# Linear attention and a bilinear FFN on one core: the order of the first units' work, and state updates moved beside the intra matmuls

## The chip, the core and the metric

The kernel runs on one core of a Trainium2 chip. The metric is device time in microseconds (us). One core has five engines that matter here: TensorE (PE in the profile; PEld are its weight loads), VectorE (DVE), ScalarE (ACT), GpSimd (POOL), and SyncE (SP), from whose queue nearly all DMAs are issued.

## The reference

The first half is decayed linear attention over 4 batches, 8 heads, 768 positions and head size 64, in blocks. The second half takes its result, as 3072 rows of 512, through a bilinear feed-forward layer (FFN).

```python
for b in range(nb):
    intra = np.einsum('bhic,bhjc->bhij', qb, kb) * Dmask[None]
    intra = np.einsum('bhij,bhjd->bhid', intra, vb)
    inter = np.einsum('bhid,bhde->bhie', qb * lam_pow[None], kv_state)
    out[:, :, sl] = intra + inter
    kb_dec = kb * rev_pow[None]
    kv_state = lam_block[None, :, None, None] * kv_state + np.einsum('bhsd,bhse->bhde', kb_dec, vb)
...
a = x @ w_a
b = x @ w_b
return (a * b @ w_out).astype(np.float32)
```

`Dmask` is lam to the power of the distance on and below the diagonal, and zero above it.

## The kernel before

**Units.** The kernel uses blocks of 128 positions, so each batch has NB = 6 blocks, and a block of one batch with all 8 heads is a unit; there are 24. q is multiplied by lam^pos and k by lam^-pos (tables lp_q and lp_k), so that the decay needs no factor in the state, which is then a plain sum of k times v over a batch's earlier units. The mask that remains is a triangle of ones (`lotri`). Heads are handled in pairs (HP = 4 pairs), 128 rows for two heads.

**The pieces of a unit.**
- `prep_k` and `prep_v` (L273, L285; P, or PK and PV, in the plan): scale q and k into `qk`, cast v into `vb`; from unit 11 on a DMA transpose on SP's queue makes `qkT`, before that `piece_T` (L289, T) does it on TensorE with a ScalarE copy. They also issue later loads (`pump`).
- `scores` (L302): k times q for each head, 16 matmuls of half the rows for two units, into two PSUM banks `kq` per unit; `masks` (L312, VectorE, L320): two multiplies by the triangle per unit, bank by bank. Both together are `piece_S` (S).
- `inter` (L330): the state `st` of the unit before times q, four matmuls; `intra` (L339): masked scores times v, eight matmuls of 64 output rows (two heads fill the two halves of the array); both add into the bank `o_ps`. `evac_o` (L349, ScalarE as a rule) copies it into `xT`, the FFN's input.
- `piece_V` (L387, V): `kv_update` (L367) adds k times v of the unit to the batch's state in the bank `kvd`, with four 128x128 matmuls (two heads by two heads), of which the two diagonal 64x64 blocks are used. `kv_copy` (L374) then copies it into `st` with a multiply by `bdiag`, which zeroes the other two blocks (VectorE, L381). The last unit of a batch has no update.
- `pieces_O` (L394; O, O2, Q in the plan): outputs of one or two units. Q also takes one or two later units `nxt`, whose scores are put between inter and intra; their masks are issued last.

**The FFN** (`ffn`, L437) works on groups of 4, 1, 2, 4, 4, 4, 4 and 1 units (GROUPS). For each of FC = 12 slices of d_ff, `a_part` (L417) makes four matmuls into a bank a_ps and a ScalarE copy, `b_part` (L423) four into b_ps and a VectorE multiply (`ab`, L425). Then each 128 rows of output take 12 matmuls (op, L434), a ScalarE copy and a store. After slice f it calls `hook(f)`; in the output part `hook(12 + 2t)` and `hook(13 + 2t)` after the first and the second half of tile t. These are the slots. What is issued in a slot stands in PLAN (L39), written out by hand: group, then (slot, piece, unit). The order within each engine is the program's order (manual scheduling), so the attention of later units is woven into the FFN of earlier ones on every engine's queue.

**Banks.** `ps_bank` (L105) hands out seven PSUM banks in rotation; FFN allocations skip the bank that the last FFN allocation took:

```python
i = bank["next"]
while i in bank["held"] or (ffn and i == bank["ffn"]):
    i = (i + 1) % 7
if ffn:
    bank["ffn"] = i
bank["next"] = (i + 1) % 7
```

A new tile in a bank waits for the readers of the tile before it. The eighth bank is that of `kvd` (and of the idle matmuls of `warm`, L192, which keep TensorE active at the start).

**The first four units** (the packed start, L487 to L582) come before any FFN. q and k of four units are loaded in a packed layout, four head pairs in two parts; `load4` (L497) scales a part on VectorE (L503), transposes it on TensorE (L508), and `unpack` (L516) copies it out on ScalarE (L517). For k the two halves of a part go into one bank, and each is unpacked by itself. `scores4` (L533) makes the scores of four units for a part (L542) and then their masks, `natural_k` (L521) transposes k back for the state updates, and `kv_mms` (L356) builds the states of units 0 to 2 in three banks at once. Then follow intra, inter and evacuations of the four units, and the FFN of group 0.

Of the kernel before, what the change touches and what calls it, by code (L numbers as in the profile page):

```python
# [17 lines left out]
BF16 = mybir.dt.bfloat16  # L18
# [4 lines left out]
def _bc(ap, dims):  # L23
# [9 lines left out]
PACK = 4  # L33
# [16 lines left out]
}  # L50
for _g, _u in ((3, 11), (4, 15), (5, 19)):
    PLAN.setdefault(_g, []).extend(
        [(1, "V", _u - 1), (1, "P", _u + 2), (3, "P", _u + 3), (4, "V", _u),
         (7, "Q", (_u, _u + 1, _u + 2, _u + 3)), (10, "V", _u + 1), (10, "P", _u + 4),
         (12, "P", _u + 5), (13, "V", _u + 2), (16, "Q", (_u + 2, _u + 3, _u + 4, _u + 5))])
PLAN[5] = [(_s, _n, (21, 22, 23) if _us == (21, 22, 23, 24) else _us)
           for _s, _n, _us in PLAN[5] if _us != 24]
PLAN[6] = [(1, "V", 22), (4, "O", 23)]


@with_exitstack
def kernel(
# [11 lines left out]
    nc = tc.nc  # L74
    B, H, S, D = q.shape
    BLK = 128
    NB = S // BLK
    HP = H // 2
# [26 lines left out]
    def ps_bank(name, shape, dt, hold=False, ffn=False):  # L105
# [6 lines that stand above are left out]
        if hold:  # L112
            bank["held"].add(i)
        return ps_pool.tile(shape, dt, name=name, tag=f"ps{i}")
# [19 lines left out]
    staged = {}  # L134
# [32 lines left out]
    n0 = GROUPS[0]  # L167
# [24 lines left out]
    def warm(n, cols=128):  # L192
        for _ in range(n):
            nc.tensor.matmul(idle_ps[:, :cols], lhsT=idle_sb[:, :128], rhs=idle_sb[:, :cols],  # L194
                             start=True, stop=True, skip_group_check=True)
# [5 lines left out]
    x4 = {}  # L201
    for w, src in (("q", q), ("k", k)):
        x4_r = src[0, :, 0:PACK * BLK, :].rearrange("h (p r) d -> p h (r d)", r=PACK)
        for i in range(2):
            t = wst_pool.tile([128, 1024], F32, name=w + "4", tag="wst")
# [42 lines left out]
    U = {}  # L248
# [81 lines left out]
    def inter(u):  # L330
        d = U[u]
        if u % NB > 0:
            first = o_bank(u)
            for hp in range(HP):
                nc.tensor.matmul(d["o"][:, hp, :], lhsT=st_bufs[(u - 1) % 4][:, hp, :, :],  # L335
                                 rhs=d["qT"][:, hp, :], start=(first and hp == 0), stop=True,
                                 skip_group_check=True)

    def intra(u):  # L339
        d = U[u]  # L340
        first = o_bank(u)
        for hp in range(HP):
            for i in range(2):
                p = slice(64 * i, 64 * i + 64)
                nc.tensor.matmul(d["o"][p, hp, :], lhsT=d["vb"][:, 2 * hp + i, :],  # L345
                                 rhs=d["m"](i, hp), start=(first and hp == 0),
                                 stop=True, skip_group_check=True)

    def evac_o(u, xT, col, eng="act"):  # L349
        o_ps = U[u].pop("o")  # L350
        if eng == "act":
            nc.scalar.copy(xT[:, :, col:col + BLK], o_ps)  # L352
        else:
            nc.vector.tensor_copy(xT[:, :, col:col + BLK], o_ps)

    def kv_mms(ps, w, hps, first):  # L356
        d = U[w]
        for hp in hps:
            nc.tensor.matmul(ps[:, hp, :, :], lhsT=d["kn"][:, 2 * hp:2 * hp + 2, :],  # L359
                             rhs=d["vb"][:, 2 * hp:2 * hp + 2, :], start=(first and hp == 0),  # L360
                             stop=True, skip_group_check=True)
# [5 lines left out]
    def kv_update(u):  # L367
        if u % NB == NB - 1:
            return
        if u % NB == 0:  # L370
            kv_bank()
        kv_mms(kv["ps"], u, range(HP), u % NB == 0)

    def kv_copy(u, ps, eng="dve"):  # L374
        st = st_bufs[u % 4]
        if eng == "act":
            for i in range(2):
                p = slice(64 * i, 64 * i + 64)
                nc.scalar.copy(st[p, :, i, :], ps[p, :, i, :])  # L379
        else:  # L380
            nc.vector.tensor_mul(st[:].rearrange("p hp i d -> p hp (i d)"),  # L381
                                 ps[:].rearrange("p hp i d -> p hp (i d)"), bdiag_bc)
# [11 lines left out]
    def pieces_O(us, nxt=()):  # L394
        kqs = [score_banks() for u in nxt]
        for u in us:
            inter(u)
        for u, kq in zip(nxt, kqs):
            scores(u, kq)
        for u in us:  # L400
            intra(u)
            xT, col = xTs[u]
            evac_o(u, xT, col)
        for u, kq in zip(nxt, kqs):
            masks(u, kq)

# [87 lines left out]
    xT4 = {"q": scr[0][:, 4:8, :], "k": scr[1][:, 4:8, :]}  # L494
    kn4 = scr[1][:, 8:12, :].rearrange("p u (h d) -> p u h d", d=D)

    def load4(w, i, parts):  # L497
        dst = xs4[w].rearrange("p r (h d) -> p r h d", d=D)
        tab = lp_q if w == "q" else lp_k
        tps = ps_bank("t" + w, [128, 2, PACK, 128], BF16)  # L500
        for j in range(2):
            hs = slice(4 * i + 2 * j, 4 * i + 2 * j + 2)
            nc.vector.tensor_mul(  # L503
                dst[:, :, hs, :].rearrange("p r h d -> p h r d"),
                x4[w, i][:, :, 2 * j:2 * j + 2].rearrange("p r h d -> p h r d"),
                tab[:, NB:, hs, :].rearrange("p r h o -> p h r o").to_broadcast([128, 2, PACK, D]))
            for r in range(PACK):
                nc.tensor.transpose(tps[:, j, r, :],  # L508
                                    xs4[w][:, r, hs.start * D:hs.stop * D], ident)
            if parts == 2:  # L510
                unpack(i, tps, slice(j, j + 1), w)
        staged.pop((w + "4", i))
        if parts == 1:
            unpack(i, tps, slice(0, 2), w)

    def unpack(i, tps, js, w):  # L516
        nc.scalar.copy(xT4[w][:, 2 * i + js.start:2 * i + js.stop, :]  # L517
                       .rearrange("c hp (p r) -> c hp p r", r=PACK),
                       tps[:, js].rearrange("c j r p -> c j p r"))

    def natural_k(us, hps):  # L521
        nu, nh = len(us), len(hps)
        tps = ps_bank("tn", [128, nu, nh, 128], BF16)
        for a, u in enumerate(us):
            for b, hp in enumerate(hps):
                nc.tensor.transpose(tps[:, a, b, :], xT4["k"][:, hp, u * BLK:(u + 1) * BLK], ident)
        nc.scalar.copy(kn4[:, us[0]:us[0] + nu, 2 * hps[0]:2 * (hps[0] + nh), :]
                       .rearrange("p u h d -> p u (h d)"),
                       tps[:].rearrange("p u j x -> p u (j x)"))

    ms4 = {}

    def scores4(i):  # L533
        kqs = []
        for up in range(PACK // 2):
            kq = score_banks()
            for uu in range(2):
                cols = slice((2 * up + uu) * BLK, (2 * up + uu + 1) * BLK)
                for j in range(2):
                    for par in range(2):  # L540
                        p = slice(64 * par, 64 * par + 64)
                        nc.tensor.matmul(kq[par][:, 2 * uu + j, :],  # L542
                                         lhsT=xT4["k"][p, 2 * i + j, cols],
                                         rhs=xT4["q"][p, 2 * i + j, cols],
                                         start=True, stop=True, skip_group_check=True)
            kqs.append(kq)
        for up, kq in enumerate(kqs):
            ms4[i, up] = mask(kq)

    for u in range(n0):  # L550
        U[u] = dict(kn=kn4[:, u], qT=xT4["q"][:, :, u * BLK:(u + 1) * BLK],
                    m=lambda i, hp, u=u: ms4[hp // 2, u // 2][i][:, 2 * (u % 2) + hp % 2, :])
    for w, parts in (("q", 1), ("k", 2)):
        for i in range(2):
            load4(w, i, parts)
            if w == "q":
                warm(4)
    for u in range(n0):
        make_vb(u, "pool")
    scores4(0)  # L560
    natural_k((0, 1, 2), (0, 1))
    natural_k((0, 1, 2), (2, 3))
    scores4(1)
    sts = [ps_bank("kv0", [128, HP, 2, D], F32), ps_bank("kv1", [128, HP, 2, D], F32), kv_bank()]
    for hh in range(2):
        for u, ps in enumerate(sts):
            for w in range(u + 1):
                kv_mms(ps, w, range(2 * hh, 2 * hh + 2), w == 0)
            if hh:
                kv_copy(u, ps, ("act", "act", "dve")[u])  # L570
    intra(0)
    evac_o(0, *xTs[0])
    intra(1)
    inter(1)
    evac_o(1, *xTs[1])
    intra(2)
# [73 lines left out]
```

## Time and profile before

| | |
|---|---|
| median of 18 runs | 238.84 us (237.87 to 242.3) |
| the profiled execution's own time | 238.44 us |
| its span, first to last instruction | 236.7 us |
| granted TensorE clock, mean | 0.989 |
| TensorE, VectorE, ScalarE busy | 228.1, 115.7, 92.7 us |
| first FFN matmul starts | 20.38 us |
| FFN matmuls a_ps, b_ps, op | 77.1, 77.2, 65.6 us |
| masks (VectorE, L320) | 48 instructions, mean 682 ns |
| state copies (VectorE, L381) | 18 instructions, mean 684 ns |

A timeline line has the start in us, the length in us, the engine, the line of the kernel, the instruction with what it writes and reads, and the number of like instructions merged into it; in brackets is idle time ahead of it and what ended it. The end of a matmul is modelled, so the start of the next one is the better measure of its cost. The chain of waits is followed back from the last instruction to whatever released each step.

### The profile page before, as it was taken

How to read it: one execution, taken by the hardware profiler on the slowest of the kernel's cores; microseconds unless marked ns; L12 is line 12 of the kernel's file. 1: busy time of each engine (PE TensorE's matmuls, PEld its weight loads, DVE VectorE, ACT ScalarE, POOL GpSimd, SP SyncE). 2: the span in 40 equal slices, each digit the busy share in tenths (PEclk: the TensorE clock that was granted, in tenths of full speed). 3: DMA queues.
4: the chain of work that ended last, by engine and by line, in shares of the span. 5: the costliest groups of instructions: out<-in, count | busy, mean ns of one | idle time of the engine just before them, and what ended most of it. 6: DMA issues, size and time to landing. Idle time of an engine off the chain costs nothing.

```text
span 236.7 us, 4519 instructions
## 1 busy us (share of the span) xinstructions
PE 228.1 (96%) x1761; PEld 126.7 (54%) x1761; DVE 115.7 (49%) x205; ACT 92.7 (39%) x174; POOL 49.2 (21%) x63
## 2 busy tenths in 40 slices
PE   7689999998999999999999999999999999999993
PEld 2375444458698754454544454544454544444493
DVE  0875656646658637675135665135564214332050
ACT  3558555046464542342143242242341233431161
POOL 6050000245346354103305403003300000000000
PEclk9979999999999999999999999999999999999998
DMA  4999999999989999996929969523120220000311
GB/s 151 302 289 348 348 367 271 295 212 288 232 193 217 204 222 228 238 175 100 226 87 216 182 78 231 139 74 80 25 47 0 89 89 4 0 0 18 118 44 48
DMA packets 94278, 38.32 MB, mean 162 GB/s; under 512 B 81200, under 2 KB 89776, under 8 KB 94256
## 3 DMA queue, kind: packets, MB, share of 16 engines
q1 hardware_dynamic: 94112, 38.02, 70.1%
q8 instruction: 14, 0.23, 0.4%
q14 instruction: 8, 0.07, 0.1%
q10 hardware_dynamic: 144, 0.00, 0.0%
HBM read 28.32 MB, written 6.29 MB: 146 GB/s over the span
## 4 chain that ended last, share of the span: by engine, by line
PE 88%; SPq 4%; ACT 2%; DMA 2%; issue 1%; DVE 1%; POOL 0%; DVEq 0%; ACTq 0%
PE a_ps L413 27%; PE b_ps L413 26%; PE op L434 26%; SPq L125 3%; PE o_ps L345 2%; DMA vf<-in_v_dram 2%; PE kq L308 2%; PE kvd L359 2%; PE o_ps L335 1%; PE tps L294 1%; ACT xT L352 1%; SPq L206 1%; ACT o_sb L429 1%; ACT st L379 1%; PE kv L359 0%
## 5 line engine op out<-in xcount | busy, mean ns | idle before, releaser
L425 DVE TENSOR_TENSOR ab<-a_sb,b_ps 128x512 bf16<-128x512 bf16 (+2 forms) x96 | 52.7, 553 | 82.5 <-PE b_ps L413 60.2
L413 PE MATMUL a_ps<-xT,wa_sb 128*128 128x512 bf16 (+2 forms) x384 | 77.1, 326 | 1.2 <-ACT xT L352 0.6
L413 PE MATMUL b_ps<-xT,wb_sb 128*128 128x512 bf16 (+2 forms) x384 | 77.2, 326 | 0.0
L420 ACT CAST a_sb<-a_ps 128x512 bf16<-128x512 f32 (+2 forms) x96 | 45.6, 481 | 66.1 <-PE a_ps L413 65.7
L434 PE MATMUL op<-wo_sb,ab 128*128 128x512 bf16 (+2 forms) x312 | 65.6, 363 | 0.0
L413 PEld LDWEIGHTS <-wb_sb 128*128 128x128 bf16 x384 | 34.5, 98 | 28.8 <-issue 0.2
L413 PEld LDWEIGHTS <-wa_sb 128*128 128x128 bf16 x384 | 33.6, 98 | 28.1 <-issue 1.4
L434 PEld LDWEIGHTS <-ab 128*128 128x128 bf16 x312 | 28.6, 98 | 30.2
L320 DVE TENSOR_TENSOR m<-kq,lotri 128x512 bf16<-128x512 f32 x48 | 29.9, 682 | 21.9 <-PE kq L308 20.4
L256 POOL TENSOR_TENSOR qk<-kf,lp_k 128x512 bf16<-128x512 f32 x17 | 17.9, 1052 | 78.1 <-issue 33.2
L429 ACT COPY o_sb<-op 128x512 f32<-128x512 f32 (+2 forms) x26 | 14.2, 554 | 37.2 <-PE op L434 37.2
L261 POOL TENSOR_TENSOR qk<-qf,lp_q 128x512 bf16<-128x512 f32 x20 | 22.9, 1144 | 24.5 <-DMA qf<-in_q_dram 24.5
L352 ACT CAST xT<-o_ps 128x512 bf16<-128x512 f32 x23 | 12.4, 590 | 16.4 <-PE o_ps L345 16.4
L381 DVE TENSOR_TENSOR st<-kvd,bdiag 128x512 bf16<-128x512 f32 x18 | 12.3, 684 | 3.8 <-PE kvd L359 3.8
L296 ACT COPY qkT<-tps 128x1024 bf16<-128x1024 bf16 x7 | 7.1, 1012 | 11.2 <-PE tps L294 11.2
L270 DVE CAST vb<-vf 128x512 bf16<-128x512 f32 x17 | 8.6, 503 | 0.0
L345 PE MATMUL o_ps<-m,vb 128*64 128x128 bf16 x192 | 7.8, 222 | 0.0
L194 PE MATMUL idle<-idle_sb 128*128 128x512 bf16 (+1 forms) x21 | 6.3, 465 | 1.3 <-DVE idle_sb L189 1.3
L270 POOL CAST vb<-vf 128x512 bf16<-128x512 f32 x7 | 4.3, 614 | 15.3 <-DMA vf<-in_v_dram 12.5
L335 PEld LDWEIGHTS <-st 128*128 128x128 bf16 x80 | 5.4, 98 | 2.8
L308 PE MATMUL kq<-qkT 64*128 64x128 bf16 x160 | 6.6, 218 | 0.0
L345 PEld LDWEIGHTS <-vb 128*64 128x64 bf16 x192 | 5.7, 109 | 1.3
(52 smaller groups left out, 86.5 us busy)
## 6 DMA issues: line engine op xcount, KB each, us to landing
vf<-in_v_dram SPq DMA_DIRECT2D x24, 256.0 KB, 5.0
out_dram<-o_sb SPq DMA_DIRECT2D x23, 256.0 KB, 2.2
qf<-in_q_dram SPq DMA_DIRECT2D x20, 256.0 KB, 4.4
kf<-in_k_dram SPq DMA_DIRECT2D x20, 256.0 KB, 4.9
wst<-in_moe_w_a_dram SPq DMA_DIRECT2D x6, 512.0 KB, 8.9
wst<-in_moe_w_b_dram SPq DMA_DIRECT2D x6, 512.0 KB, 9.0
wst<-in_moe_w_out_dram SPq DMA_DIRECT2D x6, 512.0 KB, 8.7
q<-in_q_dram SPq DMA_DIRECT2D x2, 512.0 KB, 5.6
```

The costliest lines, as they stand in the source:

```text
L256: eng_of(eng).tensor_mul(qk[:, 1], raw.pop((u, "k")), lp_k[:, u % NB].to_broadcast([128, H, D]))
L261: eng_of(eng).tensor_mul(U[u]["qk"][:, 0], raw.pop((u, "q")), lp_q[:, u % NB].to_broadcast([128, H, D]))
L270: eng_of(eng).tensor_copy(vb, vf)
L320: nc.vector.tensor_mul(m, kq[i], lotri_bc)
L345: nc.tensor.matmul(d["o"][p, hp, :], lhsT=d["vb"][:, 2 * hp + i, :], rhs=d["m"](i, hp), start=(first and hp == 0), stop=True, skip_group_c ...
L352: nc.scalar.copy(xT[:, :, col:col + BLK], o_ps)
L381: nc.vector.tensor_mul(st[:].rearrange("p hp i d -> p hp (i d)"), ps[:].rearrange("p hp i d -> p hp (i d)"), bdiag_bc)
L413: nc.tensor.matmul(ps[:, :gt], lhsT=w_sb[:, s, f * 128:(f + 1) * 128], rhs=xT[:, s, :gt], start=(s == 0), stop=(s == KS - 1))
L420: nc.scalar.copy(a_sb[:, :gt], ps[:, :gt])
L425: nc.vector.tensor_mul(ab[:, f, :gt], a_sb[:, :gt], ps[:, :gt])
L429: nc.scalar.copy(o_sb[:, lo:hi], op[:, lo:hi])
L434: nc.tensor.matmul(op[:, lo:hi], lhsT=ab[:, f, t * 128:(t + 1) * 128], rhs=wo_sb[:, f, lo:hi], start=(f == 0), stop=(f == FC - 1))
```

## The change

In the packed start, each half of a part of k gets a bank of its own and is transposed and unpacked by itself (`part_k`), with three idle matmuls of 128 columns after each of the first three halves. The first part's scores (`scores4` now takes the pairs of units to do) come ahead of the last half's transposes, and two idle matmuls after each `natural_k`. The second part's scores are issued in two steps among the state matmuls, the banks of the first two states being taken before them, and the last six state matmuls for unit 2 with its copy come after intra of unit 1.

From unit 7 on, when `pieces_O` outputs two units, the second one's state update (`kv_beside`) is issued right after their intra matmuls and ahead of the masks of `nxt`. It writes only the two diagonal blocks, with eight matmuls of 128 rows, 64 output rows and 64 columns, except for the first unit of a batch, which keeps the four full ones. The V pieces of units 8, 10, 12, 14, 16, 18, 20 and 22 leave the plan, and the S pieces of units 11 and 12 move from slot 2 to slot 3.

```diff
     2: [(0, "V", 6), (1, "T", 7), (1, "P", 8), (4, "T", 8), (5, "P", 9), (6, "S", 7),
-        (6, "S", 8), (7, "V", 7), (8, "P", 10), (9, "T", 9), (10, "V", 8), (11, "T", 10),
+        (6, "S", 8), (7, "V", 7), (8, "P", 10), (9, "T", 9), (11, "T", 10),
...
-    3: [(2, "S", 11), (2, "S", 12)],
+    3: [(3, "S", 11), (3, "S", 12)],
...
-        [(1, "V", _u - 1), (1, "P", _u + 2), (3, "P", _u + 3), (4, "V", _u),
-         (7, "Q", (_u, _u + 1, _u + 2, _u + 3)), (10, "V", _u + 1), (10, "P", _u + 4),
+        [(1, "P", _u + 2), (3, "P", _u + 3), (4, "V", _u),
+         (7, "Q", (_u, _u + 1, _u + 2, _u + 3)), (10, "P", _u + 4),
...
-PLAN[6] = [(1, "V", 22), (4, "O", 23)]
+PLAN[6] = [(4, "O", 23)]
...
+    def kv_beside(u):
+        if u % NB == 0 or u % NB == NB - 1:
+            kv_update(u)
+        for hp in range(HP if 0 < u % NB < NB - 1 else 0):
+            for i in range(2):
+                p = slice(64 * i, 64 * i + 64)
+                nc.tensor.matmul(kv["ps"][p, hp, i, :], lhsT=U[u]["kn"][:, 2 * hp + i, :],
+                                 rhs=U[u]["vb"][:, 2 * hp + i, :],
+                                 start=False, stop=True, skip_group_check=True)
+        if u % NB < NB - 1:
+            kv_copy(u, kv["ps"])
...
             evac_o(u, xT, col)
+        if len(us) == 2 and us[0] >= n0 + 3:
+            kv_beside(us[1])
         for u, kq in zip(nxt, kqs):
             masks(u, kq)
...
-    for w, parts in (("q", 1), ("k", 2)):
-        for i in range(2):
-            load4(w, i, parts)
-            if w == "q":
-                warm(4)
+    for i in range(2):
+        tps = packed_bank("q")
+        for j in range(2):
+            scale4("q", i, j)
+            transpose4("q", i, j, tps)
+        unpack(i, tps, slice(0, 2), "q")
+        warm(4)
+    for i, j in ((0, 0), (0, 1), (1, 0)):
+        scale4("k", i, j)
+        part_k(i, j)
+        warm(3)
+    scale4("k", 1, 1)
     for u in range(n0):
         make_vb(u, "pool")
-    scores4(0)
+    scores4(0, (0, 1))
+    part_k(1, 1)
     natural_k((0, 1, 2), (0, 1))
+    warm(2)
     natural_k((0, 1, 2), (2, 3))
-    scores4(1)
+    warm(2)
     sts = [ps_bank("kv0", [128, HP, 2, D], F32), ps_bank("kv1", [128, HP, 2, D], F32), kv_bank()]
-    for hh in range(2):
-        for u, ps in enumerate(sts):
-            for w in range(u + 1):
-                kv_mms(ps, w, range(2 * hh, 2 * hh + 2), w == 0)
-            if hh:
-                kv_copy(u, ps, ("act", "act", "dve")[u])
+
+    def kv_part(u, hps):
+        for w in range(u + 1):
+            kv_mms(sts[u], w, hps, w == 0)
+
+    scores4(1, (0,))
+    kv_part(0, (0, 1))
+    kv_part(1, (0, 1))
+    scores4(1, (1,))
+    kv_part(2, (0, 1))
+    for u in range(2):
+        kv_part(u, (2, 3))
+        kv_copy(u, sts[u], "act")
     intra(0)
     evac_o(0, *xTs[0])
     intra(1)
+    kv_part(2, (2, 3))
+    kv_copy(2, sts[2], "dve")
     inter(1)
```

`scale4`, `transpose4`, `packed_bank` and `part_k` are `load4` taken apart: one multiply, four transposes, a bank, and the last two with an unpack of one half.

More of the change, by code (lines that the diff above doesn't have):

```diff
@@ L495, with scale4, transpose4, packed_bank @@
     kn4 = scr[1][:, 8:12, :].rearrange("p u (h d) -> p u h d", d=D)
[L497 to L514, printed above, removed]
+    def scale4(w, i, j):
+        hs = slice(4 * i + 2 * j, 4 * i + 2 * j + 2)
+        nc.vector.tensor_mul(
+            xs4[w].rearrange("p r (h d) -> p h r d", d=D)[:, hs],
+            x4[w, i][:, :, 2 * j:2 * j + 2].rearrange("p r h d -> p h r d"),
+            (lp_q if w == "q" else lp_k)[:, NB:, hs, :].rearrange("p r h o -> p h r o")
+            .to_broadcast([128, 2, PACK, D]))
+        if j == 1:
+            staged.pop((w + "4", i))
+    def transpose4(w, i, j, tps):
+        h = 4 * i + 2 * j
+        for r in range(PACK):
+            nc.tensor.transpose(tps[:, j, r, :], xs4[w][:, r, h * D:(h + 2) * D], ident)
+    def packed_bank(w):
+        return ps_bank("t" + w, [128, 2, PACK, 128], BF16)
+    def part_k(i, j):
+        tps = packed_bank("k")
+        transpose4("k", i, j, tps)
+        unpack(i, tps, slice(j, j + 1), "k")
     def unpack(i, tps, js, w):
@@ L531, with scores4 @@
     ms4 = {}
-    def scores4(i):
+    def scores4(i, ups):
         kqs = []
-        for up in range(PACK // 2):
+        for up in ups:
             kq = score_banks()
@@ L546, in scores4 @@
             kqs.append(kq)
-        for up, kq in enumerate(kqs):
+        for up, kq in zip(ups, kqs):
             ms4[i, up] = mask(kq)
```

## The prediction

> **What bounds the kernel now.** I read the page's busy shares and chain first, then TensorE's timeline from end to end, then VectorE's beside it at the places that the change touches.
>
> ```profile
> PE 228.1 (96%) x1761; PEld 126.7 (54%) x1761; DVE 115.7 (49%) x205; ACT 92.7 (39%) x174; POOL 49.2 (21%) x63
> ...
> PE 88%; SPq 4%; ACT 2%; DMA 2%; issue 1%; DVE 1%; POOL 0%; DVEq 0%; ACTq 0%
> ```
>
> TensorE is the bound. From 20.38 us (first FFN matmul) its timeline has almost no hole, so after that the time moves only by TensorE work added or removed, or by a new wait of TensorE. Before 20.38 three engines hand work to each other; there the order decides.
>
> Startup, TensorE and VectorE timelines:
>
> ```profile
> 10.79 0.84 PE L508 MATMUL tk<-ident,scratch 128*128 128x128 bf16 x8 [0.67 <-ACT scratch L517]
> 12.34 0.38 PE L508 MATMUL tk<-ident,scratch 128*128 128x128 bf16 x4 [0.71 <-ACT scratch L517]
> 12.65 0.62 PE L542 MATMUL kq<-scratch 64*128 64x128 bf16 x16
> ...
> 13.16 4.88 DVE L320 TENSOR_TENSOR m<-kq,lotri 128x512 bf16<-128x512 f32 x8 [1.38 <-PE kq L542]
> ```
>
> Two groups of transposes wait for ScalarE to empty their own bank, and the first masks follow the scores. The stretches of 1 us then show the clock (PE busy, count, PEclk, DMA share, GB/s):
>
> ```profile
> 13.00:14.00 1.00, 1.00 (x18) 0.63 1.28 220
> 14.00:15.00 1.00, 1.00 (x16) 0.50 1.10 281
> 15.00:16.00 1.00, 0.89 (x15) 0.50 1.09 354
> 16.00:17.00 1.00, 1.00 (x15) 0.66 1.07 343
> ```
>
> Half clock from 13 + (1-0.74) = 13.26 to 16 + 0.68 = 16.68 us (0.37/0.5 = 0.74 us of the first stretch, 0.34/0.5 = 0.68 us of the last).
>
> Steady state, what one V piece (four state matmuls, one VectorE copy) costs, and what follows a Q piece in slot 7 of group 3:
>
> ```profile
> 90.55 0.39 PE L359 MATMUL kvd<-vb,qk 128*128 128x128 bf16 x4
> 90.78 1.03 PE L413 MATMUL a_ps<-xT,wa_sb 128*128 128x512 bf16 x4
> ...
> 102.11 0.62 PE L308 MATMUL kq<-qkT 64*128 64x128 bf16 x16
> 102.67 0.64 PE L345 MATMUL o_ps<-m,vb 128*64 128x128 bf16 x16
> 103.41 1.02 PE L413 MATMUL a_ps<-xT,wa_sb 128*128 128x512 bf16 x4
> ```
>
> ```profile
> 102.07 0.69 DVE L425 TENSOR_TENSOR ab<-a_sb,b_ps 128x512 bf16<-128x512 bf16 x1 [1.04 <-PE b_ps L413]
> 102.67 2.48 DVE L320 TENSOR_TENSOR m<-kq,lotri 128x512 bf16<-128x512 f32 x4
> ```
>
> A V piece takes 90.78 - 90.55 = 0.22 us of TensorE. After Q the next a_ps starts at 103.41. The first mask ends at 102.67 + 0.68 = 103.35. Sixteen intra matmuls followed by output matmuls need only 0.56 us (118.33 to 118.89), here 0.74. In groups 4 and 5 the same start is 138.77 and 173.68, and the first masks end at 138.02 + 0.68 = 138.70 and 172.94 + 0.68 = 173.62: each time 0.06 to 0.07 us after the mask. The code says why: with x the bank of the last b_ps, Q takes x+1 to x+4 for scores and x+5, x+6 for outputs; the next FFN allocation skips x and gets x+1, the bank of the first mask. **So after each slot-7 Q TensorE already waits for the first mask**, at almost no cost today. This is what the change touches.
>
> **What the Trainium skill says.** PSUM — Partial Sum Buffer, "Engine vs sequencer instructions": "ScalarE/VectorE/GpSimdE queues are strict FIFO." The trace agrees: in group 3 the masks, ready 0.43 us after the first score matmul in groups 4 and 5, start 0.56 us after it, when the ab multiply ahead of them lets go, and a_ps is late by the same 0.12 us. The same page's summary wants PSUM read in another bank than the one matmuls write: the 0.67 and 0.71 us waits above are that. TensorE: Matmul & The Clock Gate, "Part 1": the clock is set by activity in windows of about 3.4 us; the half-clock stretch above lasts 3.42 us. TensorEngine Tiling (Array Packing), "Key Properties": a change of tile shape drains the array; here 0.1 us (score matmuls at 92.60 instead of 91.64 + 0.86 = 92.50).
>
> **The change, part by part.**
>
> *Startup.* With own banks the k transposes start 0.06 us after their scaling instead of after ScalarE: groups at 9.72, 10.32, 11.23 us (VectorE ends scaling at 9.66, 10.26, 11.17, 11.77). ScalarE unpacks from 10.16, 10.75, 11.66 (0.43 us after each first transpose). The nine idle matmuls (0.056 us each, 0.5 us) fall into waits for scaling. The scores go at 11.72 instead of 12.65; masks from 11.72 + 0.51 = 12.23 instead of 13.16, one each 0.60, the fourth ends at 14.71. Then banks decide: by the rotation the third and fourth masks hold the banks that the next scores take, so these start at 14.77 (before: 14.59 to 15.75, at half clock), the next masks at 15.2 after 0.6 us of idle VectorE. State matmuls up to 16.53 (24 minus the last six); ScalarE's four state copies from 16.52 at 0.38 each, to 18.04 (before 17.23 to 18.75). Now intra of unit 1 waits for the bank of the first state (17.31), the last six state matmuls end at 17.97, unit 2 waits for the second state's bank (18.08), inter of unit 3 ends at about 19.3. Last ScalarE evacuation 19.07 + 0.44 = 19.51 to 20.10, FFN at 20.15: **gain 0.23 us**. The 0.93 us won at the masks is eaten by bank waits and by the moved state matmuls. Weights don't hinder: the first landed at 16.95, each further half megabyte takes about 1.5 us at 350 GB/s, so the third is there at 20 for a cast at 20.5. Clock: transposes, scores and idle matmuls in 9.85 to 13.26 come to about 2.0 us of array time against 1.2 before (dropped) and 1.35 in 6.4 to 9.85 (held). I take full clock; at half clock the start would be 0.6 us late. Bounds -0.6 to +0.6.
>
> *Matmuls of the state.* Eight V pieces go (units 8, 10 to 22 by twos): -8 x 0.22. Beside the intra matmuls come eight of 64 columns for units 8, 10, 14, 16, 20, 22 and the old four for 12 and 18. No row shows 64-column matmuls. Nearest: sixteen intra matmuls of the same 128*64 tile in about 0.46 us without the switch, 0.028 each. The skill (TensorE: Matmul & The Clock Gate, "Back-to-back issue gap") gives a floor of about 25 ns below 64 columns. So 8 x 0.028 = 0.22, estimated; low 0.11 (pairs at half of 56 ns), high 0.45 (no pairing). At 0.22 this is a swap, worth nothing. The tile shape is intra's, and the switch back was paid before.
>
> *The copy ahead of the masks.* In a Q piece the state's VectorE copy (L381) is queued before the four masks, and waits for matmuls that TensorE issues only after both units' intra. Behind it: four masks, then FFN multiplies; TensorE waits for mask one. With I the first intra: state matmuls at I + 0.46 (I + 0.57 with the switch, unit 12), copy 0.43 later (113.12 to 113.55 on an idle VectorE), mask one 0.60 after that, its end +0.68, a_ps +0.06. That is I + 2.23 for units 16 and 20, I + 2.34 for 12, against I + 0.63, 0.62, 0.74 today: +1.60, +1.61, +1.60 = +4.81. The three V pieces gone at slot 10 give back 0.67. **Slot 7: +4.14** (3.8 to 4.8). The wait for the second mask is covered by the a_ps work of 0.86.
>
> *Slot 16* (units 14, 18): the second half of the output tile, 6 x 0.216 = 1.30, stands before the next bank. It ends at I + 0.78 + 1.30 = I + 2.09, mask one at 2.23 and 2.34: +0.14 and +0.25. Group 5 scores one unit only, so bank x+1 isn't reached by that allocation (it takes x+5): 0. **+0.39** (0.1 to 0.8).
>
> *Slot 12 of group 2.* Next bank wanted at 83.40, mask one done at 83.34: no wait. But unit 9's copy now stands behind unit 8's copy and the late masks:
>
> ```profile
> 81.29 0.64 PE L345 MATMUL o_ps<-m,vb 128*64 128x128 bf16 x16
> ...
> 83.17 0.39 PE L359 MATMUL kvd<-vb,qk 128*128 128x128 bf16 x4
> 83.39 1.46 PE L434 MATMUL op<-wo_sb,ab 128*128 128x512 bf16 x6
> 84.69 0.61 PE L335 MATMUL o_ps<-qkT,st 128*128 128x128 bf16 x8
> ```
>
> Unit 8's matmuls start at 81.86 - 0.22 = 81.64, its copy at 82.06, masks 82.66 to 85.06, the v cast 0.34, unit 9's copy 85.40 to 86.09; inter of unit 10 can start at 86.15 instead of 84.92. **+1.24** at the following intra (86.46 for 85.22); 1.0 to 1.5.
>
> *The rest at nothing.* S of units 11 and 12 one slot later: four masks of 2.4 us, read at slot 7, over 6 us on. V at slots 1 and 10 gone frees 0.68 us of VectorE where TensorE didn't wait. No piece moved issues a DMA; nothing moves past SP's or POOL's queue. Cover for unit 10's copy: the output half (1.3 us) and the whole next group.
>
> Sum: -0.23 + 4.14 + 0.39 + 1.24 = +5.54. The profiled run took 238.44 (span 236.7 and 1.7 around it), giving 243.98; the median of the runs is 0.40 higher, so **244.4 us**.
>
> **Rivals.** *Faster:* the start of a_ps after Q isn't bound to the mask but is a drain of the tile switch; then copy and masks run under 0.86 us halves and only gains stay: 0.23, and 0.11 for each of six 64-column updates: 238.84 - 0.23 - 0.66 = 237.95. It decides if a_ps follows the last kvd within 0.15 us. Against it: three starts 0.06 to 0.07 us behind the mask, and the bank arithmetic. *No change:* the swap is worth nothing, the startup gain is lost to half clock, and no mask delays anything: 238.8. *Slower still:* 64-column matmuls don't pair, six times 0.23 more: 245.8. Nothing speaks for this but that no row shows it. *Not doing what it says* in part: the idle matmuls don't hold the clock; 244.4 + 0.8 = 245.2, inside the first case's range.
>
> **How the numbers follow.** Delayed masks 0.78 (own range 242.5 to 246.0), slower still 0.10, faster 0.08, no change 0.04. Low end: 0.4 off the slot-7 sum, 0.2 off slot 12, 0.3 off slot 16, 0.4 of cheaper matmuls and 0.4 more at startup make 242.7, taken as 242.5; high end with unpaired matmuls and some of the startup loss 246.5. A measurement of this kernel tells about 0.2% (0.5 us) from no change. Faster 0.08, same 0.04, slower 0.88.
>
> **What would show it.** Right: in group 3 to 5 the masks after a slot-7 Q start about 1.5 us after the first intra, with one L381 copy ahead; a_ps starts 2.2 to 2.3 us after the first intra; inter of unit 10 stands alone 1.2 us after that of unit 9; kvd x8 takes 0.22 us; PEclk 1.00 from 13 to 17 us; FFN at 20.1. Wrong: a_ps within 0.8 us of the intra group, kvd groups of 0.4 us, or an FFN start before 19.5.

## The result and the profile after

The changed kernel takes 243.08 us (median of 8 runs, 242.78 to 243.81) against 238.58 us (48 runs) before: **1.0192** times as long, 95% interval 1.0173 to 1.0211, or +4.50 us. The prediction was 244.4 us, slower. The profiled execution took 243.11 us, its span is 241.3.

TensorE's busy line and the line on TensorE's waits in the chain, from the page of the changed kernel:

```profile
PE 227.2 (94%) x1798; PEld 125.7 (52%) x1798; DVE 117.5 (49%) x205; ACT 92.8 (38%) x174; POOL 48.0 (20%) x63
...
PE 87%; DVE 5%; DMA 3%; ACT 2%; issue 1%; SPq 1%; DVEq 0%; ACTq 0%
```

TensorE is busy 0.9 us less than before (228.1), though the span is 4.6 us longer. The 0.9 us lie ahead of 20 us (16.2 us busy before, 15.0 after); from there on TensorE is busy for 211.9 and 212.1 us. So the longer span is waiting and not work. VectorE's share of the chain of waits went from 1% to 5%. Who TensorE waited for, in all (us in total, times, longest):

```profile
PE a_ps L427 <- DVE m L320: 4.2, 3, 1.4
...
PE o_ps L335 <- DVE st L393: 1.0, 1, 1.0
```

Neither line is among the waits of the kernel before. The first is the wait behind the slot-7 Q piece, in each of groups 3 to 5. TensorE, then VectorE, in group 3:

```profile
102.86 0.62 PE L308 MATMUL kq<-qkT 64*128 64x128 bf16 x16
103.41 0.64 PE L345 MATMUL o_ps<-m,vb 128*64 128x128 bf16 x16
103.98 0.40 PE L359 MATMUL kvd<-vb,qk 128*128 128x128 bf16 x4
105.76 1.04 PE L427 MATMUL a_ps<-xT,wa_sb 128*128 128x512 bf16 x4 [1.39 <-DVE m L320]
```

```profile
104.41 0.69 DVE L393 TENSOR_TENSOR st<-kvd,bdiag 128x512 bf16<-128x512 f32 x1 [0.91 <-PE kvd L359]
105.02 2.48 DVE L320 TENSOR_TENSOR m<-kq,lotri 128x512 bf16<-128x512 f32 x4
```

VectorE stands idle for 0.91 us although the scores are finished, because the copy at the head of its queue waits for the state matmuls. Then come the copy and mask one, which ends at 105.02 + 0.68 = 105.70; a_ps starts 0.06 us later. From the first intra matmul that is 2.35 us, against 0.74 before. The second line is in group 2:

```profile
84.36 0.39 PE L335 MATMUL o_ps<-qkT,st 128*128 128x128 bf16 x4
85.74 0.40 PE L335 MATMUL o_ps<-qkT,st 128*128 128x128 bf16 x4 [0.99 <-DVE st L393]
86.06 0.64 PE L345 MATMUL o_ps<-m,vb 128*64 128x128 bf16 x16
86.54 0.29 PE L380 MATMUL kvd<-vb,qk 128*64 128x64 bf16 x8
86.76 1.47 PE L448 MATMUL op<-wo_sb,ab 128*128 128x512 bf16 x6
```

Inter of unit 9 runs, inter of unit 10 waits for unit 9's state. The last two lines give the price of the 64-column updates: from the first intra matmul to the next output matmul 0.70 us, with only 0.58 (85.22 to 85.80) before, so eight of them cost 0.12 us.

Start times on TensorE in both profiles show where the time went ("step" is what was added since the row above):

| place | before | after | later by | step |
|---|---|---|---|---|
| first FFN matmul | 20.38 | 20.18 | -0.20 | -0.20 |
| a_ps of group 3 | 87.10 | 88.06 | 0.96 | +1.16 |
| a_ps after Q, slot 7, group 3 | 103.41 | 105.76 | 2.35 | +1.39 |
| a_ps of group 4 | 122.79 | 125.22 | 2.43 | +0.08 |
| a_ps after Q, slot 7, group 4 | 138.77 | 142.50 | 3.73 | +1.30 |
| a_ps of group 5 | 157.70 | 161.71 | 4.01 | +0.28 |
| a_ps after Q, slot 7, group 5 | 173.68 | 178.99 | 5.31 | +1.30 |
| a_ps of group 6 | 192.84 | 198.06 | 5.22 | -0.09 |
| last output matmuls | 230.18 | 235.18 | 5.00 | -0.22 |

The step of -0.22 in the last row is the V piece of unit 22, which is gone from slot 1 of group 6. The span grew by 4.6 only, less than the 5.0 of the last row: from the start of the last output matmuls to the end of the last store it is 6.5 us in the profile before and 6.1 after, with the same code. Why is not shown.

### The profile page after: what moved, and what is told of

The parts are those of the page before. It is cut to its first block, busy times and chain, and to the rows that moved or that the text cites. A ratio compares the mean times of both kernels' runs of the same rounds, so it can differ in the third digit from the quotient of the medians.

```text
span 241.3 us, 4568 instructions
## 1 busy us (share of the span) xinstructions
PE 227.2 (94%) x1798; PEld 125.7 (52%) x1798; DVE 117.5 (49%) x205; ACT 92.8 (38%) x174; POOL 48.0 (20%) x63
## 4 chain that ended last, share of the span: by engine, by line
PE 87%; DVE 5%; DMA 3%; ACT 2%; issue 1%; SPq 1%; DVEq 0%; ACTq 0%
PE a_ps L427 26%; PE b_ps L427 26%; PE op L448 24%; DMA k<-in_k_dram 3%; DVE m L320 3%; PE o_ps L345 3%; PE kq L308 2%; PE o_ps L335 2%; DVE st L393 1%; PE kvd L359 1%; PE tps L294 1%; ACT o_sb L443 1%; SPq L206 1%; ACT xT L352 0%; PE kq L560 0%
## 5 line engine op out<-in xcount | busy, mean ns | idle before, releaser
L261 POOL TENSOR_TENSOR qk<-qf,lp_q 128x512 bf16<-128x512 f32 x20 | 21.8, 1089 | 24.1 <-DMA qf<-in_q_dram 24.1
L270 DVE CAST vb<-vf 128x512 bf16<-128x512 f32 x17 | 10.1, 596 | 0.0
L194 PE MATMUL idle<-idle_sb 128*128 128x128 bf16 (+1 forms) x34 | 6.8, 332 | 1.3 <-DVE idle_sb L189 1.3
L335 PE MATMUL o_ps<-qkT,st 128*128 128x128 bf16 x68 | 5.8, 219 | 1.0 <-DVE st L393 1.0
```

What stands on the lines that cost most here:

```text
L261: eng_of(eng).tensor_mul(U[u]["qk"][:, 0], raw.pop((u, "q")), lp_q[:, u % NB].to_broadcast([128, H, D]))
L270: eng_of(eng).tensor_copy(vb, vf)
```

## The experiments

The theory on trial: the VectorE copy ahead of the masks makes mask one late, and with it the bank that TensorE wants next (the mask theory). The rivals: the place and shape of the state matmuls on TensorE; VectorE's load rather than its order; the startup. The ratios are to the kernel before, with 95% intervals.

**The halves.** `startup_only` has the new packed start with the plan and the output pieces of before; `steady_only` the reverse.

> Only the first half of the change: the new order of the packed start, with the plan and the output pieces of the kernel before. The mask theory (the whole loss sits in the Q pieces) expects 0.2 us less than the kernel before, about 238.4 us, with the first FFN matmul at 20.2 us. A rival that puts part of the loss into the startup (bank waits of the new rotation carried into later groups) expects 239 or more.

> Only the second half of the change: state updates beside the intra matmuls and the new plan, with the packed start of the kernel before. The mask theory expects the whole loss and the 0.2 us of the startup besides, about 243.3 us. If the halves aren't additive (the startup's shift decides whether copies collide), it lies under 242.5.

Measured: 238.04 us, ratio 0.9991 (0.9972 to 1.0010), first FFN matmul at 20.14 us; and 243.64 us, 1.0210 (1.0181 to 1.0238). The loss sits wholly in the second half. The first half's gain of 0.2 us in the trace is too small for its interval. In `steady_only`'s profile the first FFN matmul starts only at 21.32: with the same old start, the clock is at half for 6.8 us there (11.4 to 18.2), against 3.4 in the kernel before. So its median of 4 runs isn't fine enough to tell whether the halves add up exactly.

**The copy to ScalarE.** The state matmuls stay beside intra, the copy leaves VectorE's queue:

```diff
-            kv_copy(u, kv["ps"])
+            kv_copy(u, kv["ps"], "act")
```

> The changed kernel, but the state copy of the update beside the intra matmuls goes to ScalarE (two copies of a diagonal half each, 0.38 us apiece) instead of VectorE; the matmuls stay where the change put them. The mask theory: nothing stands ahead of the masks, so the first mask is early again, a_ps starts about 0.70 us after the first intra matmul in slot 7 (2.15 to 2.35 in the changed kernel), inter of unit 10 doesn't wait, and what stays are the startup's 0.2 us and about 0.1 us for each 64-column update: about 237.9 us. The rival theory, that the state matmuls in the output piece are what costs (their place on TensorE and tile shape), expects 243 us as in the changed kernel.

Measured: 237.36 us, ratio **0.9947** (0.9927 to 0.9967): 5.7 us under the changed kernel and faster than the kernel before. TensorE, then ScalarE, at the same place in group 3:

```profile
102.56 0.64 PE L345 MATMUL o_ps<-m,vb 128*64 128x128 bf16 x16
103.13 0.40 PE L359 MATMUL kvd<-vb,qk 128*128 128x128 bf16 x4
103.37 1.03 PE L427 MATMUL a_ps<-xT,wa_sb 128*128 128x512 bf16 x3
```

```profile
103.02 1.07 ACT L352 CAST xT<-o_ps 128x512 bf16<-128x512 f32 x2 [1.40 <-PE o_ps L345]
103.98 0.75 ACT L391 CAST st<-kvd 64x256 bf16<-64x256 f32 x2
104.75 0.58 ACT L434 CAST a_sb<-a_ps 128x512 bf16<-128x512 f32 x1
```

The state matmuls are where the change put them, and a_ps follows them at once, 0.81 us after the first intra matmul instead of 2.35. The next a_sb copy starts 1.38 us after a_ps does, where it was 1.06 before (104.47 behind 103.41), and nobody on TensorE waits for it. The rival that the matmuls' place costs is out. This run also takes work off VectorE; the next one does not.

**The copy behind the masks.** VectorE does all it did, in another order:

```diff
         for u, kq in zip(nxt, kqs):
             masks(u, kq)
+        if len(us) == 2 and us[0] >= n0 + 3 and us[1] % NB < NB - 1:
+            kv_copy(us[1], kv["ps"])
```

(and the copy in `kv_beside` goes).

> The changed kernel, but the state copy of the update beside the intra matmuls is issued on VectorE after the masks of the output piece instead of ahead of them. The mask theory: the waits in slot 7 and slot 16 go (about 4.4 us of the loss); in group 2 a new one comes, since the state matmuls of unit 9 in slot 13 must wait until unit 8's copy, now behind four masks, has read the bank: about 1.0 us at slot 13 in place of the wait of inter of unit 10. Sum about 238.8 us. The rival that it is the matmuls' place expects 243 us; a rival that it is VectorE's load, not its order, expects 243 us too.

Measured: 238.10 us, ratio 0.9974 (0.9957 to 0.9990). The same VectorE work in another order takes 5.0 us less than the change, so it is order and not load. In slot 7 of group 3 a_ps follows again at once, 0.80 us after the first intra matmul:

```profile
103.80 0.64 PE L345 MATMUL o_ps<-m,vb 128*64 128x128 bf16 x16
104.37 0.40 PE L359 MATMUL kvd<-vb,qk 128*128 128x128 bf16 x4
104.60 1.03 PE L427 MATMUL a_ps<-xT,wa_sb 128*128 128x512 bf16 x3
```

The new wait came where it was expected, in slot 13 of group 2:

```profile
81.86 0.29 PE L380 MATMUL kvd<-vb,qk 128*64 128x64 bf16 x8
82.31 1.24 PE L448 MATMUL op<-wo_sb,ab 128*128 128x512 bf16 x5 [0.16 <-issue]
84.40 0.39 PE L359 MATMUL kvd<-vb,qk 128*128 128x128 bf16 x4 [0.85 <-DVE st L391]
```

Unit 9's matmuls find the bank `kvd` still unread. `last_v8` puts unit 8's update back into slot 10:

> As copy_last (VectorE copy after the masks), but unit 8's update goes back to slot 10 of group 2 as in the kernel before. If the wait of unit 9's state matmuls in slot 13 (0.85 us in copy_last) is what copy_last has left of the loss, it goes: 0.85 less and 0.1 more for the full matmuls, about 237.4 us. If copy_last's rest lies elsewhere, 238.1 us.

Measured: 237.69 us, 0.9964 (0.9940 to 0.9988); the wait is gone (unit 9's matmuls at 83.46, right behind the output half). The medians are 0.41 us apart where 0.75 was expected; the sign is right, but the intervals overlap.

**The bank.** Only the choice of the bank after a slot-7 Q piece is changed; the copy stays ahead of the masks:

```diff
         for u, kq in zip(nxt, kqs):
             masks(u, kq)
+        if us[0] in (11, 15, 19):
+            bank["ffn"] = None
```

> The changed kernel, copy still ahead of the masks, but after the three slot-7 output pieces the bank rotation is told to forget the last FFN bank, so that the next a_ps takes the bank of the last b_ps, which no mask reads; b_ps then takes the first mask's bank. If the wait is for the first mask's bank, a_ps starts 0.7 to 0.8 us after the first intra matmul, b_ps waits until about 2.15 to 2.35, and each piece gives back one half of 0.86 us: 3 x 0.86 = 2.6, about 240.5 us. If TensorE waits for something else in the output piece (the copy itself, or the state matmuls), nothing moves: 243 us.

Measured: 240.72 us, ratio 1.0076 (1.0059 to 1.0094), 2.36 us under the changed kernel.

```profile
103.81 0.64 PE L345 MATMUL o_ps<-m,vb 128*64 128x128 bf16 x16
104.39 0.40 PE L359 MATMUL kvd<-vb,qk 128*128 128x128 bf16 x4
104.62 1.03 PE L429 MATMUL a_ps<-xT,wa_sb 128*128 128x512 bf16 x4
106.17 1.04 PE L429 MATMUL b_ps<-xT,wb_sb 128*128 128x512 bf16 x4 [0.52 <-DVE m L320]
```

a_ps starts 0.81 us after the first intra matmul, and b_ps, which now has mask one's bank, waits: the stall follows the bank. This is the direct evidence of what TensorE waits for.

**The copy twice.** In `kv_beside` the line with `kv_copy` stands two times.

> The changed kernel with the VectorE state copy beside the intra matmuls issued twice (the second writes the same values). The mask theory expects 0.60 us more for each place where TensorE waits: three slot-7 pieces, slot 16 in groups 3 and 4, inter of unit 10: 6 x 0.6 = 3.6 us more, about 246.7 us. If only the wait for the state matmuls counts and not the copy's length, about 243 us.

Measured: 249.37 us, ratio 1.0418 (1.0377 to 1.0460), 6.3 us more than the changed kernel instead of 3.6. The wait of a_ps in group 3 grew from 1.39 to 2.11 us. VectorE, then TensorE:

```profile
105.56 1.42 DVE L394 TENSOR_TENSOR st<-kvd,bdiag 128x512 bf16<-128x512 f32 x2 [0.92 <-PE kvd L359]
106.89 2.48 DVE L320 TENSOR_TENSOR m<-kq,lotri 128x512 bf16<-128x512 f32 x4
```

```profile
107.63 1.04 PE L428 MATMUL a_ps<-xT,wa_sb 128*128 128x512 bf16 x4 [2.11 <-DVE m L320]
```

The first mask starts 1.33 us after the first copy instead of 0.60, so the second copy adds 0.73 us and not 0.60. That makes 3 x 0.72 in slot 7, 2 x 0.72 in slot 16, and 1.0 between the first intra and the second one of group 2, together 4.6. The rest is this, in TensorE's busy time by stretches (clock in the column behind the count):

```profile
178.00:182.00 4.00, 3.65 (x58) 1.00 0.23 31
182.00:186.00 4.00, 2.24 (x8) 0.86 0.52 39
186.00:190.00 4.00, 4.00 (x15) 0.71 0.00 0
190.00:194.00 4.00, 4.00 (x20) 1.00 0.00 0
```

After the wait in group 5 the clock is halved for (0.14 + 0.29) x 4 / 0.5 = 3.4 us, which costs 1.7 us. The mean clock is 0.993 in all four runs of this kernel, which fits one such loss in each. Thus the length of the copy counts in full, as the mask theory says, and a stall of 2.1 us can have a second price: it followed one of the three such waits in the profile. In the changed kernel (1.39 us) no stretch shows it.

**The shape of the state matmuls.** `full_beside` is the changed kernel with `kv_update` (four full matmuls) for every unit; `act_full` is the same on top of `copy_act`, where no mask waits.

> The changed kernel, but the update beside the intra matmuls always uses the four full 128x128 matmuls instead of eight of 64 columns. The trace of the changed kernel puts the eight at about 0.12 us and the copy's start 0.2 us earlier; so the full ones should cost 0.2 us more at units 8, 14, 16 and 20 and 0.1 at units 10 and 22: about 1.0 us more than the changed kernel, 244.1 us. If 64 columns cost as much as 128 (the recorded estimate of 0.22 us each), 243.1 us.

> As copy_act (state copy beside the intra matmuls on ScalarE), but with four full 128x128 state matmuls for every unit instead of eight of 64 columns. No mask waits for the copy here, so this prices the tile shape alone: if eight 64-column matmuls save about 0.1 us at each of units 8, 10, 14, 16, 20 and 22, it is 0.6 us above copy_act, about 238.0 us; if the shape is worth nothing, 237.4 us.

Measured: 244.51 us, 1.0232 (1.0187 to 1.0277), 1.4 us above the changed kernel, though the intervals of the two ratios overlap; and 238.35 us, 0.9978 (0.9959 to 0.9997), against 0.9947 (0.9927 to 0.9967) for `copy_act`. The trace of `full_beside` is closer to what was expected: a_ps comes 2.35 us after the first intra matmul in all three slot-7 pieces (2.15 with 64 columns), and the last output matmuls start 0.82 us later than in the changed kernel. TensorE in the Q piece of group 4, first `act_full`, then `copy_act`:

```profile
138.09 0.64 PE L345 MATMUL o_ps<-m,vb 128*64 128x128 bf16 x16
138.66 0.40 PE L359 MATMUL kvd<-vb,qk 128*128 128x128 bf16 x4
138.89 1.03 PE L426 MATMUL a_ps<-xT,wa_sb 128*128 128x512 bf16 x3
```

```profile
137.78 0.64 PE L345 MATMUL o_ps<-m,vb 128*64 128x128 bf16 x16
138.25 0.29 PE L380 MATMUL kvd<-vb,qk 128*64 128x64 bf16 x8
138.48 1.04 PE L427 MATMUL a_ps<-xT,wa_sb 128*128 128x512 bf16 x3
```

From intra to a_ps it is 0.80 against 0.70 us. From the first intra matmul of units 7 and 8 (80.92 and 80.95) to the last output matmuls (230.04 and 229.44) the two differ by 0.63 us, so the shape is worth 0.10 us at each of six units. In single medians the difference is larger (1.0 us), but they come from two sets of runs, and the intervals of their ratios overlap.

**Steady state with ScalarE copies, old start.**

> The second half of the change with the state copy on ScalarE, and the packed start of the kernel before. Against the kernel before it holds only the cheaper state updates: six times 0.1 us less, about 238.0 us. If copy_act's whole gain of 0.53% was the new start, 238.6 us.

Measured: 237.55 us, ratio 0.9968 (0.9946 to 0.9990). The intervals of this run and `copy_act` overlap, so the medians don't settle which half makes the gain. The traces do for theirs: from the first FFN matmul to the last output matmuls it is 209.80 us before, 209.79 in `act_full`, 209.33 in `copy_act` and 209.36 here. Of the 0.74 us by which `copy_act`'s last output matmuls start sooner than before, 0.47 come from the 64-column updates and 0.27 from the start.

**The idle matmuls.** The new start alone, without the thirteen idle matmuls that the change adds.

> Only the new packed start (plan and output pieces of before), without the new idle matmuls (the nine after the k halves and the four after the back-transposes left out). If the idle matmuls hold the clock, it falls to half from about 13.2 us and the first FFN matmul is 0.6 to 0.8 us later than with them: about 238.8 us against 238.0. If the closer packing of real matmuls alone holds the clock, 238.0 us.

Measured: 238.45 us, ratio 0.9991 (0.9974 to 1.0009), the same as with them. Clock (behind the count) by stretches of 1 us, without them:

```profile
13.00:14.00 1.00, 0.51 (x6) 1.00 1.23 208
14.00:15.00 1.00, 0.61 (x11) 1.00 1.06 277
15.00:16.00 1.00, 1.00 (x21) 1.00 1.05 351
16.00:17.00 1.00, 0.81 (x17) 1.00 1.10 350
```

Full clock where the kernel before had half, and the first FFN matmul at 20.01 us, earlier than with them (20.14). In this profile the closer packing of real matmuls was enough, and the clock of all runs agrees: the median of the runs' mean clocks is 0.993 for the kernel before (34 runs), and above 0.999 for the new start, with idle matmuls (14 runs) and without (22).

## Why the prediction was right, point by point

**The copy ahead of the masks in slot 7** was predicted at +1.60, +1.60 and +1.61 us for groups 3, 4 and 5, before the V pieces are taken off; the trace has 2.35 - 0.74 = 1.61, 2.15 - 0.63 = 1.52 and 2.15 - 0.62 = 1.53. `copy_act`, `copy_last` and `bank_x` each take away one link (the copy, its place, the bank), and the stall goes or moves. The Trainium skill's sentence that VectorE's queue is strict FIFO (PSUM — Partial Sum Buffer, "Engine vs sequencer instructions") carried this step, and the 0.91 us of idle VectorE in front of finished scores shows it.

**Slot 16** was predicted at +0.14 and +0.25; the output matmuls up to the next a_ps take 4.06 instead of 3.90 us in group 3 and 4.15 instead of 3.89 in group 4: +0.16, +0.26. (The working's I + 2.09 should be 2.08 by its own terms, which changes nothing.)

**Slot 12 of group 2** was predicted at +1.24 to the intra of units 9 and 10, counted without the startup's gain. It is 86.06 - 85.22 = 0.84, and with the startup's 0.20 back 1.04: right in kind (inter of unit 10 waits for unit 9's copy), 0.2 too long. About 0.1 of this is a slip in the working: it put unit 8's matmuls at 81.64, where the old output matmuls would have begun, tile switch included, although it had counted none for slot 7 (I + 0.46). They start 0.47 us after the first intra matmul (81.31 - 80.84). The other 0.1 is the shorter update below.

**The term that was mis-sized is the 64-column update**: "At 0.22 this is a swap, worth nothing". Eight of them take 0.12 us, near the low bound of 0.11. At units 10 and 22 this shortens TensorE's path by 0.10 us each. At units 8, 14, 16 and 20 TensorE waits for VectorE soon after, and what counts is that the copy starts sooner: 141.15 - 140.35 = 0.80 us after the first intra matmul, for the 0.89 of the prediction. So a_ps comes at I + 2.15 in groups 4 and 5, for the predicted 2.23; with the four full matmuls, `full_beside` has 2.35 there. The nearest row had misled: 0.028 us per intra matmul is 0.056 per pair, but this scales with the 128 columns; at 64 a pair takes about 0.03. The floor of 25 ns in the Trainium skill (TensorE: Matmul & The Clock Gate, "Back-to-back issue gap"), which was taken for each instruction, doesn't hold here for two matmuls side by side in the array: 0.12 us for eight is 15 ns each.

**The startup** was predicted at -0.23 (20.15 us) and is -0.20 (20.18), with the waits where the working had them: scores at 14.12 and 14.72 behind masks, intra of unit 1 at 17.31 behind the first state's copy. What wasn't right is its reading of the clock: the idle matmuls were credited with a part in holding it, and the profile without them holds it as well. Its own count allowed for that: 2.0 us of array time less 0.5 of idle matmuls is still above the 1.35 that had held. That the size fits so well is in part luck, because the old start itself varies: its first FFN matmul is at 20.38 us in the profile before, at 20.27 in `act_old_start` and at 21.32 in `steady_only`.

**The sum** of 5.54 stands against 5.00 at the last output matmuls. The 64-column term explains 0.2 by itself and about 0.3 through the earlier copies, and the slip in slot 12 another 0.1; slot 16 and the startup came out 0.03 us or so over. The rest of the way from 244.4 down to 243.08 us is of two kinds: the last 6 us of the kernel were 0.4 us shorter in this profile, and the prediction added 0.40 us because the median of 18 runs lay that far above the profiled run, while for the changed kernel the median (243.08) and the profiled run (243.11) agree. The faster rival (a_ps held up only by the tile switch) fell with the first trace: a_ps comes 1.78 us after the first kvd matmul in group 3, and not behind the last one.

## What to carry to other kernels

Work added to an in-order queue is paid by what stands behind it: before putting an instruction that waits ahead of others, look at who wants the results behind it, and which bank or buffer they hold. A rotation of banks turns a late reader into a stall of the bound engine, even when the engine of that reader is idle half of the time (VectorE is busy for 49% of the span here). Moving the small copy to a queue with nothing urgent behind it (here ScalarE) kept the gain of 64-column updates beside the intra matmuls, and made the change 0.53% faster than the kernel before instead of 1.9% slower.

## What the runs showed of the hardware that wasn't expected

Eight matmuls of 64 output rows and 64 columns, in pairs on the two halves of the array, took 0.12 us, with 0.1 us more for the switch back to the full array. A TensorE wait of 2.12 us in `copy_twice` was followed by 3.4 us at half clock, from about 1.1 us after matmuls had resumed; two waits of 2.11 us in the same profile, and the waits of 1.39 us in the changed kernel's, weren't. One of the six runs of `full_beside`, whose waits are as long as the changed kernel's, took 247.03 us at a mean clock of 0.993 (the others 0.998 to 1.0); it has no trace, so whether a wait lost the clock there is open. A second VectorE copy into the same 128x512 tile starts 0.73 us after the first, while a mask behind a copy starts after 0.60.
